# A gated linear attention and gMLP kernel on one core: constants made by separate operations, more engines per operation, a full-row bias matmul, and another order table

## The chip, the core and the metric

One Trainium2 chip, one of its cores. The core has five engines that run their own instruction queues in order and wait for one another by semaphores: TensorE (PE in the profile, its weight loads PEld), VectorE (DVE), ScalarE (ACT), GpSimd (POOL) and SyncE (SP), which here issues almost all DMA transfers. The metric is the device time of one execution in microseconds (us), as the median of several runs; lower is better.

## What is computed

Two stages follow each other. The first is a recurrence over time for 4 batches and 8 heads, 768 steps, head size 48; the second a gated MLP with a matmul along the sequence.

```python
# q, k, v, alpha: (4, 8, 768, 48)
for t in range(S):
    state = alpha[:, :, t, :, None] * state + np.einsum('bhd,bhe->bhde', k[:, :, t], v[:, :, t])
    y[:, :, t] = np.einsum('bhd,bhde->bhe', q[:, :, t], state)
x = y.transpose(0, 2, 1, 3).reshape(B, S, H * D)          # (4, 768, 384)
h = np.maximum(x @ w_in, 0.0)                             # w_in: (384, 1024)
u, v = h[..., :512], h[..., 512:]
v_n = (v - mean(v)) / np.sqrt(var(v) + 1e-06)             # over the last axis
v_s = np.einsum('ts,bsd->btd', w_spatial, v_n) + b_spatial[None, :, None]   # 768 x 768
out = (u * v_s) @ w_out                                   # w_out: (512, 384)
```

## The kernel before

**Chunks.** Each batch's 768 steps are cut into 6 chunks of 128, so there are 24 chunks, numbered 0 to 23 through all batches. Inside a chunk the recurrence is done as masked attention: logarithm of alpha (`ln`), cumulative sums by a matmul with a triangle of ones (`cum`), exponentials of both signs (`einv`, `eexp`), products with k (`kt`) and q (`qt`), transposes of both (`tr`, `trk`) and copies out of PSUM (`ev`, tile kqT), scores (`sc`), the causal mask (`m`, tile ptm), and the output `y`; across chunks a state is carried by `upd`, `z`, `S` and `sb` (tile sbd). The result is copied (`xs`), transposed (`xt`) and copied again (`xe`). Chunks 0 to 7 are taken in pairs, two steps to a partition (`pair`, lines 423 to 632: `lnp`, `cump`, `einvp`, `ktp`, `qtp`, `vbp`, `updq`, `ya`); the others one by one (`first`, from line 634).

**The MLP.** For every chunk `v` (three matmuls of 512 columns), statistics (`bn`), `rs` (two small activations) and `vn`; for each half batch (`th`) and quarter of the features (`ft`, `dsl`) `u` (three matmuls of 384 columns), `s` (six matmuls with the transposed spatial weights, in two parts of three), then an add of the bias on DVE and the gate `g`; for each of 6 row tiles `o` (four matmuls) and its store. The last `s` of all starts with a matmul that puts the bias row into PSUM, so that its gate reads PSUM directly. In two cases (`ACT_STATS`: batch 1 chunks 4 and 5, batch 2 chunks 2 and 3) the statistics are on ACT, by sums and squares. The weights are loaded as float32, cast by any engine (`cast`), the spatial ones transposed (`wt`) and copied out (`we`).

**The order is written out.** The program first lists operations without emitting them: each call of `op` appends one, with the engines that may run it and a price for each, the operations it depends on and a priority. `dma` appends two, the issue and the transfer. Then `replay` walks the string `PLAN`: a word such as `D56` emits operation number 56 of that list on DVE; letters are P, D, A, G (POOL), S (SP) and Q (the transfer, which emits nothing). Each engine's queue is therefore the order of its words. Numbers after colons on a P word are columns of matmuls on a constant tile `junk`, run on the operation's PSUM bank ahead of it; they compute nothing that is used. PSUM is handed out as a ring of 8 banks in the order of the P words. The prices, priorities and dependencies served whoever wrote the table; at run time only the order and the semaphores count, which the framework derives from the tiles that are read and written.

**Constants.** Four operations make them: `consts` (all of `constants`, on POOL by name, but with part of its instructions on DVE), `cz 0` and `cz 1` on DVE, `cz 2` on POOL. On POOL that gives le_pair, lt_pair (the triangles for pairs), ident, mask2 in that order, and later mask4 and ut_ones, which the single chunks use.

Of the kernel before, what the change touches and what calls it, by code (L numbers as in the profile page):

```python
# [36 lines left out]
class Slot:  # L37
# [5 lines left out]
    "kt": {"POOL": 0.9},  # L43
    "vb": {"POOL": 0.48, "ACT": 0.42},
# [6 lines left out]
    "o": {"ACT": 0.4},  # L51
# [6 lines left out]
S34 Q35 S36 Q37 G32 G0 Q33 S38 Q39 S94 Q95 S40 Q41 A42 P53:512:512:192 A54 D1 D2 D56 P43 S96 Q97 S98 Q99 S100 Q101  # L58
S163 Q164 S4 Q5 S165 Q166 S167 Q168 P59:464 G58 G48 A44 A45 A55 D46 D57 D47 P249:304 P49 P61 A50 P51 D52 D60 A62 A102
A250 P71:304 P74 P113 P103 D72 D73 D76 D75 P63 P77:172 D65 A114 D116 P119:148 A104 A64 A115 A105 A78 G66 G67 G106 D107  # L60
D117 D68 P79 P81 P111 P121 P247 P109 G3 G69 A108 A82 A80 D120 D122 D112 D110 P83 A84 A171 D248 S169 Q170 S9 Q10 S307
Q308 P131 P134 D133 D136 D132 D135 G70 G118 P172:228 P182 P123:240 A183 A8 A173 A124 P137 P138 A139 A174 G7 G6 D125
P85 G126 D128 D185 G127 G129 G175 P88 P142 P140 A86 A184 D176 D186 A143 A89 P188 P190 P180 P144 P178 A141 A191 A145
A181 P146 G11 G12 S309 Q310 S311 Q312 D130 D87 D179 D90 D189 P157 A187 A177 A158 A147 A13 P197 P200 P192 D199 D201
D198 D194 D202 P151:196 P155 A315 A193 A91 P326 P316 A327 P203 P153 P204 G195 G196 G329 A317 A328 A318 P149 A205 A154
D159 D156 D152 D330 G319 P208 P334 A209 P206 D320 P332 P324 P210 P322 D92 D335 D325 D333 D148 A207 P212 A211 A150 P347
P215 P221 A213 A160 A222 A216 S14 Q15 P223 P227 S18 Q19 D93 D323 D161 D348 D349 D214 G16 G17 A224 A228 P225 P229 A226
A21 P232 A234 D231 D230 D233 G20 P235:300 P238 S313 Q314 G331 G321 P344 P336 S367 Q368 S369 Q370 S22 Q23 S371 Q372
A237 A236 D217 D162 D346 A240 D338 A239 A218 D219 D220 A375 A337 P251 P263 P259 P376 A377 A378 G339 P264 D345 D341
D265 P260 D261 P255 P252 A380 A25 A24 D381 D253 P256 D257 G340 G342 G379 S409 Q410 S373 Q374 S446 Q447 S411 Q412 S413  # L70
Q414 S415 Q416 S26 Q27 S480 Q481 S448 Q449 S482 Q483 S450 Q451 S484 Q485 P383 A385 A417 S452 Q453 S577 Q578 S486 Q487
S581 Q582 S579 Q580 S583 Q584 P244 P241 P350 A246 D384 D245 D242 D243 P390 P354 P418 D392 D391 A351 A355 G262 G343
A420 A382 G254 G266 P279 P352 P271 P356 P393 P272 A353 A357 A419 G421 A422 A394 P280 P361 P386 P275 P395 A362 A424
A396 A31 D273 D423 D281 D387 P425 D397 D427 D426 D363 G282 G388 P276 P358 D277 P398 G258 G389 G278 G30 A399 A454 A359
A28 A488 P405 P432 P267 P455 P401 A402 A457 A456 D29 P291 P489 P268 A490 A459 D406 D433 D400 D434 D360 P283 P428 D269
D460 A492 D429 D493 G458 G491 P435 A284 A292 A436 G274 G461 G270 G430 G431 S648 Q649 S617 Q618 S650 Q651 S611 Q612
S652 Q653 S613 Q614 S690 Q691 S615 Q616 S694 Q695 S654 Q655 S692 Q693 P287 P462 P437 P495 P403 D463 D464 D497 D496
A288 A439 A438 P440 A585 A441 A364 D404 P469 P498 P295 P465 P586 P303 D471 D470 D466 D500 D499 A296 A587 A588 A590
A304 P299 G494 G467 G468 G589 G592 D591 D442 P472 A473 P501 P407 P474 A502 A300 P503 P593 P596 A443 A505 A408 D475
D476 P477 A478 D504 D366 D594 D595 D445 D444 D597 D365 P506 P600 P515 D601 D516 A507 A479 A508 D509 D602 A656 A510  # L80
A619 P517 P525 P513 P519 P529 P657 P533 P620 D511 D512 P526 P530 A514 A659 A658 A621 A661 A622 A698 A624 D518 D520
D527 D531 D662 P545 P534 P699 A701 A700 A703 D625 G598 G599 G660 G626 G623 G528 D535 P546 D547 P630 P627 P664 P537
P603 D631 D665 D704 G548 A629 A628 G632 G663 A604 P538 P634 P605 S728 Q729 S762 Q763 S696 Q697 S730 Q731 S732 Q733
S764 Q765 S766 Q767 D539 A607 A666 A606 D635 D636 P541 P667 P542 G702 G532 P706 P671 D668 D543 D673 D672 G669 G536
G670 G544 G633 P608 P637 P521 A707 A736 A708 A638 P737 P713 P639 P522 P549 D714 D715 D641 D523 A770 A609 A705 A738
A739 G740 A640 A741 D742 P771 P550 P642 A772 P709 P744 A774 A643 A746 D710 D551 D775 D745 D644 G524 S858 Q859 S734
Q735 S929 Q930 S860 Q861 G773 G711 G552 G712 G743 G540 P716 P674 A717 A675 P561 P718 P676 P777 P553 A562 A678 A677
D719 D779 D720 D610 P679 P751 A778 A554 A866 A680 A645 A681 P780 D752 P747 D748 D753 D781 D782 P682 P867 P721 P754
A868 A869 A871 A722 A755 S768 Q769 S862 Q863 A723 A776 D683 D872 P573 P688 P684 G749 G750 G870 P756 P874 D646 D757
D875 D685 D758 A689 A574 D724 A876 P686 P783 P569 P881 A784 P785 A570 A787 A687 A725 D882 D786 D883 P759 P557 A760  # L90
P788 P565 P796 P798 P800 S1042 Q1043 S971 Q972 S892 Q893 S864 Q865 S898 Q899 S896 Q897 A979 A558 A789 A566 A937 A900
S894 Q895 S935 Q936 G873 S975 Q976 S931 Q932 S933 Q934 S973 Q974 S977 Q978 S1008 Q1009 S567 Q568 S1046 Q1047 S559 Q560
S1012 Q1013 S1010 Q1011 S1044 Q1045 S1014 Q1015 D727 D647 D761 D726 P794 P806 D790 A791 D799 D797 D795 D792 D793 D801
P901 P980 P802 P938 P877 P807 A902 A903 A907 A905 A981 A939 A940 A982 A944 A984 P810 P803 A942 G904 D878 G941 G879
D808 D906 D804 G805 G880 G809 G983 D985 D943 P822 P884 P811 D812 A885 P823 P908 P886 P945 D824 P814 P911 P815 D912
D909 D816 G813 G817 G913 G825 A910 A887 A888 A947 A946 P889 A1016 A890 P952 P915 P987 D953 D916 D954 P830 P1017 P831
P818 A988 A1019 A1050 A1018 D917 P948 P819 P1051 D949 A1021 A986 A989 D1022 D832 G950 P834 A1052 G951 G1020 P990 P842
P918 A835 A1054 D820 D991 D1055 A843 A919 P838 P1024 P994 P920 D1025 D921 D995 D996 A839 A1023 G914 G833 G1053 G992
S1048 Q1049 S575 Q576 S836 Q837 S844 Q845 S293 Q294 S289 Q290 S571 Q572 S305 Q306 S301 Q302 S555 Q556 A922 A1026 S297
Q298 S285 Q286 S840 Q841 P826 P955 P827 D828 A956 P1057 P957 P1031 D958 P1027 D1028 D1033 D1032 P997 P923 A1058 A1059  # L100
A959 P969 P1060 A1056 A998 P999 D1062 D1001 D1061 D970 G821 G829 G993 G1029 A1000 A924 P960 P846 P1034 A961 A847 G1030
P1063 A1035 A1064 P1002 P963 P1036 P1065 D925 D891 A1003 D962 D1066 P850 P967 A1067 A1037 D1004 A926 D928 P1068 A964
A1038 P1039 D927 D968 A851 A1005 A1069 A1040 D1006 D1041 D1007 D1070 P965 P854 P1076 P1080 P1078 P1074 D966 A1079 A855
A1071 A1081 D1075 D1072 D1073 D1077 P1094 P1082 P1106 P1086 P1083 P1098 P1095 P1090 P1102 P1087 P1107 P1091 P1103
P1110 P1099 P1111 D1096 D1084 G1085 D1088 D1097 D1108 D1092 D1093 G1089 P1113 D1104 G1109 G1105 D1112 D1100 D1101
P1117 P1121 S852 Q853 S563 Q564 S856 Q857 S848 Q849 A1114 S1115 Q1116 A1118 P1133 S1119 Q1120 A1122 P1125 A1134 S1123
Q1124 P1129 S1135 Q1136 A1126 P1137 S1127 Q1128 A1130 A1138 S1131 Q1132 S1139 Q1140
# [16 lines left out]
def kernel(  # L124
# [113 lines left out]
    def constants(_):  # L238

        nc.vector.memset(junk, 0.5)  # L240
        nc.gpsimd.memset(le_pair, 0.0)
        nc.vector.memset(mask2[:, 0].bitcast(FP32), 0.0)
        zero_padding(lap_bufs[0])
        nc.vector.memset(ones_col, 1.0)
        nc.vector.memset(halves_of, 0.0)
        for ci in range(2):
            nc.vector.memset(halves_of[64 * ci:64 * ci + 64, ci:ci + 1], 1.0)
        nc.vector.memset(lt_pair.bitcast(FP32), 0.0)
        for t, base in ((le_pair, 0), (lt_pair, 1)):
            nc.gpsimd.affine_select(  # L250
                out=t, in_=t, compare_op=ALU.is_gt, fill=1.0, base=base, channel_multiplier=1,
                pattern=[[-1, 128]],
            )
            nc.gpsimd.memset(t[0:64, 64:128], 0.0)
        for t in (ktp_bufs[0], qtp_bufs[0]):
            zero_padding(t)
        make_identity(nc, ident)
        nc.vector.memset(mask2[:, 1].bitcast(FP32), 0.0)
        for par in range(2):
            for ci in range(2):  # L260
                rows = slice(64 * ci, 64 * ci + 64)
                nc.gpsimd.affine_select(
                    out=mask2[rows, par], in_=mask2[rows, par], compare_op=ALU.is_gt, fill=1.0,
                    base=par, channel_multiplier=2, pattern=[[0, 4], [-1, 2], [-2, 64]],
                )
# [891 lines left out]
```

## Time and profile before

| | us |
|---|---|
| median of 3 runs (143.01 to 143.22) | 143.06 |
| the profiled execution | 143.08 |
| its span in the profile | 141.3 |
| TensorE busy | 133.2 |
| DVE busy | 118.3 |
| ACT busy | 108.6 |
| POOL busy | 83.4 |

The span runs from the first to the last instruction; the rest of the execution's time lies around it. Busy is the time in which at least one instruction of that engine was running; TensorE's matmuls overlap, and their ends are modelled, so a busy TensorE need not be at its peak rate. A line such as "L828 PE MATMUL bank<-vn ... x192 | 36.8, 326" names the line of the program, engine, operation, what is written and read, the count, the busy time of all and the mean of one in ns; that mean is longer than the time from one start to the next where instructions overlap. L828 is the helper of all large matmuls, L197, L199, L203 and L205 those of copies and relu.

### The profile page before, as it was taken

Reading aid. Unit: us, or ns where it says so; the run is one execution under the profiler, and the core shown is the slowest. Engines: PE = TensorE matmul, PEld = TensorE weight load, DVE = VectorE, ACT = ScalarE, POOL = GpSimd, SP = SyncE. Lnnn points to the kernel's source line nnn. Section 1 sums busy time; section 2 is a strip of 40 time slices with the busy share of each in tenths; the row PEclk is TensorE's granted clock in tenths of the full one; section 3 lists DMA queues with packets and bytes.
Section 4 is the critical chain, followed back from the end, with each engine's and each line's share of the span. In section 5 each row is a group of like instructions: output and inputs, shape, how many; then the busy total and the mean of one; then the engine's idle time right before and its main releaser. Section 6 shows DMA issues by size and latency. Waiting matters only on the chain.

```text
span 141.3 us, 4968 instructions
## 1 busy us (share of the span) xinstructions
PE 133.2 (94%) x1912; PEld 84.2 (60%) x1923; DVE 118.3 (84%) x291; ACT 108.6 (77%) x282; POOL 83.4 (59%) x146
## 2 busy tenths in 40 slices
PE   7989798999999999999999999999999989999990
PEld 3457575575667656565675665656666656566560
DVE  7479878999989599999998898989979779894940
ACT  3677569988989969889887999997889969940061
POOL 6722986293449596982299899500799993000720
PEclk9999999999999999999999999999999999999999
DMA  4999999999898989989799999979978690112044
GB/s 102 323 323 332 331 272 311 225 320 238 241 232 156 283 161 208 205 161 212 154 205 179 193 217 177 222 143 195 250 151 203 225 375 24 70 56 102 0 164 170
DMA packets 89000, 28.64 MB, mean 203 GB/s; under 512 B 83728, under 2 KB 87440, under 8 KB 88976
## 3 DMA queue, kind: packets, MB, share of 16 engines
q1 hardware_dynamic: 88944, 28.32, 81.6%
q8 instruction: 15, 0.25, 0.7%
q14 instruction: 9, 0.07, 0.2%
q0 software_dynamic: 32, 0.00, 0.0%
HBM read 23.60 MB, written 4.72 MB: 200 GB/s over the span
## 4 chain that ended last, share of the span: by engine, by line
PE 71%; DVE 9%; POOL 7%; issue 5%; ACT 4%; ACTq 0%; POOLq 0%; DVEq 0%
PE bank L828 47%; PE bank L187 4%; DVE ptm L594 3%; PE bank L719 2%; PE bank L754 2%; POOL sbd L199 2%; POOL gT L989 2%; PE bank L511 2%; PE bank L782 2%; DVE ptm L765 2%; PE bank L740 1%; PE bank L583 1%; POOL kt L690 1%; PE bank L666 1%; DVE kqT L199 1%
## 5 line engine op out<-in xcount | busy, mean ns | idle before, releaser
L828 PE MATMUL bank<-w_spT,vn 128*128 128x384 bf16 x192 | 36.8, 326 | 0.0
L989 POOL TENSOR_TENSOR gT<-vsb,uT 128x384 bf16<-128x384 f32 x28 | 25.7, 923 | 14.9 <-DVE vsb L976 14.4
L690 POOL TENSOR_TENSOR kt<-kc,binv 128x384 bf16<-128x384 f32 x16 | 14.6, 914 | 13.4 <-ACT bc L685 8.6
L765 DVE TENSOR_TENSOR ptm<-bank,mask 128x512 bf16<-128x512 f32 x32 | 20.7, 682 | 1.9 <-PE bank L398 1.2
L828 PEld LDWEIGHTS <-vn 128*128 128x128 bf16 x192 | 16.6, 97 | 9.5 <-issue 0.2
L976 DVE TENSOR_TENSOR vsb<-bank,bsp_bc 128x384 f32<-128x384 f32 x31 | 16.5, 551 | 4.2 <-PE bank L828 2.5
L828 PE MATMUL bank<-xT,w_in 128*128 128x384 bf16 x96 | 18.7, 326 | 0.0
L828 PE MATMUL bank<-w_out_sb,gT 128*128 128x384 bf16 (+1 forms) x100 | 18.7, 319 | 0.0
L828 PE MATMUL bank<-w_in,xT 128*128 128x512 bf16 x61 | 17.2, 379 | 0.8 <-issue 0.2
L344 POOL TENSOR_TENSOR state<-state,bc 128x192 f32<-128x192 f32 x20 | 10.4, 520 | 11.4 <-DVE state L337 5.4
L197 ACT COPY kqT<-bank 128x512 bf16<-128x512 bf16 x21 | 12.1, 599 | 3.9 <-PE bank L719 1.1
L199 POOL CAST sbd<-state 64x192 bf16<-64x192 f32 x38 | 13.3, 350 | 2.0
L893 DVE BATCH_NORM_STATS2 stats<-v_sb 128x6 f32<-128x512 bf16 x20 | 13.7, 683 | 0.3 <-ACT v_sb L203 0.3
L203 ACT ACTIVATE v_sb<-bank 128x512 bf16<-128x512 f32 x20 | 11.8, 605 | 1.4 <-PE bank L828 1.3
L197 ACT CAST x_sb<-bank 128x384 bf16<-128x384 f32 x24 | 11.4, 490 | 1.5 <-PE bank L623 1.3
L828 PEld LDWEIGHTS <-w_in 128*128 128x128 bf16 x96 | 8.8, 97 | 5.9
L828 PEld LDWEIGHTS <-gT 128*128 128x128 bf16 x100 | 8.9, 97 | 5.6 <-DVE gT L989 0.4
L199 DVE COPY kqT<-bank 128x512 bf16<-128x512 bf16 x27 | 10.5, 416 | 1.9 <-PE bank L511 1.0
L187 PE MATMUL bank<-junk 128*128 128x512 f32 (+9 forms) x24 | 10.2, 529 | 1.1 <-DVE junk L240 1.1
L594 DVE TENSOR_TENSOR ptm<-bank,mask 128x512 bf16<-128x512 f32 x16 | 10.2, 683 | 0.5 <-PE bank L583 0.4
L197 ACT COPY xT<-bank 128x192 bf16<-128x192 bf16 (+1 forms) x26 | 9.4, 379 | 1.6 <-PE bank L398 1.1
L197 ACT COPY o_sb<-bank 128x384 f32<-128x384 f32 x9 | 4.4, 484 | 8.0 <-PE bank L828 8.0
(126 smaller groups left out, 284.0 us busy)
## 6 DMA issues: line engine op xcount, KB each, us to landing
ac<-in_alpha_dram SPq DMA_DIRECT2D x16, 192.0 KB, 4.1
kc<-in_k_dram SPq DMA_DIRECT2D x16, 192.0 KB, 4.8
qc<-in_q_dram SPq DMA_DIRECT2D x16, 192.0 KB, 4.1
vc<-in_v_dram SPq DMA_DIRECT2D x16, 192.0 KB, 3.8
raw_w<-in_moe_w_spatial_dram SPq DMA_DIRECT2D x3, 768.0 KB, 6.8
out_dram<-raw_w SPq DMA_DIRECT2D x11, 192.0 KB, 2.5
out_dram<-o_sb SPq DMA_DIRECT2D x9, 192.0 KB, 1.8
ac<-in_alpha_dram SPq DMA_DIRECT2D x4, 384.0 KB, 5.0
```

The costliest lines, as they stand in the source:

```text
L187: nc.tensor.matmul(out=flat[:, 0:cols].rearrange("p (a b) -> p a b", a=4), lhsT=junk, rhs=junk[:, None, 0:n].to_broadcast([128, 4, n]), st ...
L197: nc.scalar.copy(out=out, in_=in_)
L199: ENG[eng].tensor_copy(out=out, in_=in_)
L203: nc.scalar.activation(out=out, in_=in_, func=AF.Relu)
L344: ENG[eng].tensor_tensor(out=st["state"], in0=st["state"], in1=st["bc"][:, :, None].to_broadcast([128, HP, D]), op=ALU.mult)
L594: nc.vector.tensor_tensor(out=st[f"ptm{par}"][:, s], in0=st[f"pt{s}{par}"], in1=mask2[:, par], op=ALU.mult)
L690: ENG[eng].tensor_mul(out=k_blocks(kt3)[:, :, :, 0:D], in0=quad(st["kc"]), in1=st["binv"])
L765: nc.vector.tensor_tensor(out=st["ptm"][:, s], in0=st[f"pt{s}"], in1=mask4, op=ALU.mult)
L828: return lambda ps: nc.tensor.matmul(out=out(ps), lhsT=lhsT(), rhs=rhs(), start=start, stop=stop)
L893: nc.vector.bn_stats(out=stats, in_=d["v_sb"][:, tt, :])
L976: nc.vector.tensor_tensor(out=hold["vs"], in0=ps[:, 0:TH], in1=bsp_bc[:, th, :], op=ALU.add)
L989: ENG[eng].tensor_tensor(out=bt[b]["gT"][:, dsl, cols], in0=hold["vs"], in1=bt[b]["uT"][:, dsl, cols], op=ALU.mult)
```

## The change

Four things are edited, and the order table is replaced as a whole. The two lumps of constants become 20 operations of their own, each with the things that need it as its dependants (the diff shows a few of these dependencies). More engines may run `kt`, `vb`, `o`, `xs`, `g`. The last bias matmul multiplies the identity with the bias already spread over 128 rows (`bsp_bc`), and so waits for that copy. The numbers of operations move by up to 15, so that the two tables can't be compared word by word.

```diff
 ENGINES = {
-    "kt": {"POOL": 0.9},
-    "vb": {"POOL": 0.48, "ACT": 0.42},
+    "kt": {"POOL": 0.9, "DVE": 0.47},
+    "vb": {"POOL": 0.48, "ACT": 0.42, "DVE": 0.27},
...
-    "o": {"ACT": 0.4},
+    "o": {"ACT": 0.4, "DVE": 0.47},
 }
...
 PLAN = """
-S34 Q35 S36 Q37 G32 G0 Q33 S38 Q39 S94 Q95 S40 Q41 A42 P53:512:512:192 A54 D1 D2 D56 P43 S96 Q97 S98 Q99 S100 Q101
...
+D0 S49 Q50 D17 D13 S109 Q110 G47 Q48 D5 S53 Q54 G10 D7 S51 Q52 D2 D3 D11 G18 D15 D12 D1 S55 Q56 A57 G14 S111 Q112 G16
+P58:512:512:192 P264 A59 P68 A60 S113 Q114 G9 A69 D62 A70 D6 P66:512:232 S115 Q116 D71 P262 A67 D4 P74 A117 D61 S178
...
-    def constants(_):
-
-        nc.vector.memset(junk, 0.5)
...
+    def triangle(t, pattern, base=0, step=1):
+
+        nc.gpsimd.affine_select(
+            out=t, in_=t, compare_op=ALU.is_gt, fill=1.0, base=base, channel_multiplier=step, pattern=pattern)
...
+    def c_tri(_):
+        nc.gpsimd.memset(le_pair, 0.0)
+        for t, base in ((le_pair, 0), (lt_pair, 1)):
+            triangle(t, [[-1, 128]], base)
+            nc.gpsimd.memset(t[0:64, 64:128], 0.0)
+
+    def c_m2(par):
+
+        def emit(_):
+            for ci in range(2):
+                triangle(mask2[64 * ci:64 * ci + 64, par], [[0, 4], [-1, 2], [-2, 64]], par, 2)
+        return emit
...
-        op(("xs", i), "ACT", 0.38, xs, got(("y", i), ("xt", i - WK)), prio=P + 9, use=[st["sl_y"]])
+        op(("xs", i), {"ACT": 0.38, "DVE": 0.47}, None, xs, got(("y", i), ("xt", i - WK)), prio=P + 9, use=[st["sl_y"]])
...
-            op(("cump", j, par), "PE", 0.33 + 0.1, cum, got(("lnp", j)), prio=P + 2, take=sl_c[par], cols=768)
+            op(("cump", j, par), "PE", 0.33 + 0.1, cum, got(("lnp", j), ("c_tri",)), prio=P + 2, take=sl_c[par], cols=768)
...
-                lambda ps: ps[:, 0:TH], lambda: ones_row, lambda: b_sp_sb[:, th * TH:(th + 1) * TH], True, False))
+                lambda ps: ps[:, 0:TH], lambda: ident, lambda: bsp_bc[:, th, :], True, False))
...
-            op(("g", b, dsl, th), {"POOL": 0.9} if b < B - 1 else {"POOL": 0.9, "DVE": 0.69}, None, gm, got(("s", b, dsl, th)), prio=Q)
+            op(("g", b, dsl, th), {"POOL": 0.9, "DVE": 0.47}, None, gm, got(("s", b, dsl, th)), prio=Q)
...
-    op(("consts",), "POOL", 4.0, constants, prio=-10.0)
-    op(("cz", 0), "DVE", 1.7, zeros(0), prio=-5.0)
-    op(("cz", 1), "DVE", 0.7, zeros(1), prio=-4.0)
-    op(("cz", 2), "POOL", 1.2, zeros(2), [made[("consts",)]], prio=-3.0)
+    op(("c_junk",), "DVE", 0.17, lambda _: nc.vector.memset(junk, 0.5), prio=-20.0)
...
+    op(("c_m4",), "POOL", 0.95, c_m4, prio=-8.0 if PAIRS else -18.0)
+    op(("c_sbd",), "DVE", 0.62, c_sbd, prio=-9.5)
+    op(("c_row",), "DVE", 0.22, c_row, prio=-9.4)
...
+        op(("c_tri",), "POOL", 1.15, c_tri, got(("c_half",)), prio=-20.5)
```

Read back into operations (a pair or chunk behind the name, then the parity of the step; junk columns in brackets), the queues begin as follows. TensorE and POOL:

```
PE before:   cump 0.1 [512+512+192], cump 0.0, tr k 0.1 [464], bias 1 [304], tr k 0.0, tr q 0.1, tr q 0.0, sc 0.0 [304], sc 0.1,
             cump 1.1, cump 1.0, updq 0, ya 0 [172], tr k 1.1 [148], xt 0, y 1, tr q 1.0, tr q 1.1, bias 0, tr k 1.0, xt 1, sc 1.0
PE after:    cump 0.0 [512+512+192], bias 1, cump 0.1, tr q 0.0 [512+232], bias 0, tr k 0.1, cump 1.1 [492], cump 1.0, tr q 0.1,
             tr k 0.0, tr k 1.1 [512+108], sc 0.0, updq 0, tr q 1.0, tr k 1.0, sc 0.1, tr q 1.1, sc 1.1 [512+500], sc 1.0, ya 0
POOL before: b_sp issue, consts, vbp 0.1, vbp 0.0, S 0, sb 0, ktp 1.0, cz 2, S 1, sb 1, vbp 1.1, two casts of w_in
POOL after:  b_sp issue, c_m4, c_m2 1, c_tri, c_m2 0, c_id, ktp 1.1, vbp 0.0, ktp 1.0, S 0, vbp 1.0, sb 0, ktp 2.1, ktp 2.0,
             S 1, c_ut, sb 1, S 2, sb 2, vbp 2.0, S 3, sb 3, cast w_in, S 4, sb 4, cast w_in
```

DVE, ACT and the loads that SP issues:

```
DVE before:  cz 0, cz 1, ktp 0.1, ktp 0.0, qtp 0.1, qtp 0.0, ev q 0.0, ev k 0.1, four m of pair 0, z 0, ktp 1.1, qtp 1.0, ...
DVE after:   11 constants, qtp 0.0, c_qt, ktp 0.1, c_la, ktp 0.0, qtp 0.1, ev k 0.1, vbp 0.1, ev k 0.0, ev q 0.1, qtp 1.1,
             qtp 1.0, two m of pair 0, z 0, two m, z 1, two m of pair 1, two casts of w_in, two m, qtp 2.0, qtp 2.1, bn 0,
             z 2, ev q 2.1, ev q 2.0, z 3, bn 1, xs 2, xs 3, z 4, four m of pair 2, ...
ACT before:  lnp 0, einvp, einvp, eexpp, eexpp, ev k 0.0, ev q 0.1, lnp 1, bias copy 1, einvp 1.1, einvp 1.0, ebcp 0, ...
ACT after:   lnp 0, einvp, eexpp, einvp, eexpp, ev q 0.0, lnp 1, both bias copies, einvp 1.1, eexpp, einvp, eexpp, ev k 1.1,
             lnp 2, ebcp 0, ev q 1.0, ev q 1.1, ev k 1.0, vbp 1.1, cast w_in, xs 0, xs 1, einvp 2.1, ...
SP before:   ac0 kc0 qc0 ac2 vc0 kc2 qc2 vc2 ac4 w_in1 kc4 qc4 vc4 w_in0 ac6 kc6 qc6 w_sp0 w_sp1 vc6 ac8 kc8 w_sp2
SP after:    ac0 ac2 qc0 kc0 vc0 kc2 qc2 vc2 ac4 w_in1 kc4 qc4 vc4 ac6 w_in0 qc6 kc6 w_sp0 w_sp1 vc6 ac8 kc8 qc8 w_sp2
```

Over the whole kernel both tables have the same 24 `sc`, 64 parts of `s`, and so on; what differs is the engine of some 60 operations, the places, and the junk: 3572 columns before, 4312 after, the last of them ahead of the first `v` after the change.

## The prediction

> **What bounds the kernel now.** I read the page's busy shares first, then the table by stretches, then the timeline of the first 16 us, the chain of waits, and the answers for single tiles.
>
> ```profile
> span 141.3 us, 4968 instructions
> PE 133.2 (94%) x1912; PEld 84.2 (60%) x1923; DVE 118.3 (84%) x291; ACT 108.6 (77%) x282; POOL 83.4 (59%) x146
> ```
>
> The table by stretches:
>
> ```profile
> 10.00:15.00 5.00, 4.11 (x114) 3.28 (x105) 4.76 (x10) 3.45 (x10) 1.97 (x5) 1.00 1.13 332
> 15.00:20.00 5.00, 4.51 (x126) 3.40 (x123) 4.39 (x9) 3.44 (x8) 4.53 (x11) 1.00 1.05 297
> 40.00:60.00 20.00, 19.90 (x309) 12.55 (x309) 17.95 (x44) 16.91 (x44) 16.21 (x26) 1.00 0.97 204
> 120.00:138.00 18.00, 17.99 (x118) 10.23 (x109) 13.28 (x31) 7.45 (x22) 3.85 (x4) 1.00 0.22 81
> ```
>
> Columns after the stretch: length, then busy time of PE, PEld, DVE, ACT, POOL, granted clock, DMA share, GB/s. From 40 us on TensorE is covered all the time; before, it is DVE that is covered and TensorE has holes, some plugged with matmuls on `junk`. Busy time hides how far it is from full, so I lay TensorE's real work end to end. Prices are start-to-start times in its unbroken stretches:
>
> ```profile
> 69.99 1.97 PE bank L828 x12
> ...
> 120.12 17.56 PE bank L828 x105
> ```
>
> That is 0.164 us for a matmul of 384 columns (1.97/12); by other pieces of the same chain 0.22 for one of 512, 0.33 to 0.35 for a score operation, 0.23 for a transpose operation of k and q, 0.51 for `ya`, 0.78 for a full `updq`, 0.17 to 0.37 for `y`. All real operations together make 120.8 us. Taking an operation's start minus the work in front of it gives the time lost so far: 4.9 us at the first real matmul, 13.5 at 30 us, 15.0 at 44 us (`trk` of chunk 8), 16.9 at the last; then 3.6 us for the last copy, store and close. So the first 44 us lose 10.1 us after the start, and the 94 us behind them only 1.9. Only the head has much to give; the rest can lose more easily than win.
>
> ```profile
> 1.22 0.67 POOL L1101 DMA_DIRECT2D b_sp_sb<-in_moe_b_spatial_dram  x1 [0.78 <-POOLq L1141]
> ...
> 2.63 0.29 POOL L250 TENSOR_SCALAR_AFFINE_SELECT lt_pair<-lt_pair 128x128 bf16<-128x128 bf16 x1
> ...
> 3.58 2.82 POOL L262 TENSOR_SCALAR_AFFINE_SELECT mask<-mask 64x512 bf16<-64x512 bf16 x4
> ...
> 4.24 0.84 ACT L452 ACTIVATE la<-ac 128x768 bf16<-128x768 f32 x1 [2.22 <-DMA ac<-in_alpha_dram]
> ...
> 5.14 0.65 PE L461 MATMUL bank<-la,le_pair 128*128 128x384 bf16 x3
> ...
> 6.18 1.09 DVE L483 TENSOR_TENSOR kt<-kc,binvp 128x384 bf16<-128x384 f32 x2 [1.95 <-ACT binvp L469]
> ...
> 9.42 0.86 ACT L452 ACTIVATE la<-ac 128x768 bf16<-128x768 f32 x1
> ```
>
> The triangles are ready (3.1 us) long before the logarithm (5.1); the loads set the pace: landings by issue and time to landing are 4.2, 5.4, 6.6, 7.8, 9.1, 10.3, 11.5, 12.7, 14.1 us for the first nine, w_in's first half 17.2, its second 24.1.
>
> **Operations that change kind.** The constants are the same instructions regrouped. The last bias row is a matmul of 384 columns with 128 rows for one with 1 row: both take the columns' 0.164 us, and the rows of before are 0.331 (1 row) and 0.326 (128 rows) for one; zero. Counting the two tables: DVE gives up 7 copies of kqT (0.416), 9 relu (0.546), 2 kt (0.566), an sbd pair and a bias copy, -10.1 us, and takes 13 PSUM copies of o and x (0.548, the bsp_bc row), 4 more casts, 2 vb, a gate and small ones, +11.1. ACT +8.8 -9.5, POOL +3.5 -2.8. Totals hardly move (119, 108, 84 us), so the order decides. A weight cast on DVE is shown for 384 elements only (0.35); bounds for 512 are 0.35 and ACT's 0.61, for 768 0.35 and POOL's 0.83; I take 0.45 and 0.55, as 384 is faster there than on POOL (0.50). The five together: 1.75 to 3.7, taken 2.55.
>
> **The head, stepped through in the new order.** Each operation starts when its engine is free and its inputs are there, with the rows' start-to-start times (ACT 0.43 for 384, 0.49 for kqT; DVE 0.6 per mask, 0.54 kt, 0.48 qt, 0.36 kqT, 0.83 for statistics; POOL 0.91 kt, 0.5 state, 0.72 sbd) and about 0.1 between engines.
>
> 1. POOL runs b_sp's issue (to 1.9), mask4 (0.95), half of mask2 (1.41), and only then the triangles (1.25): 5.55. First real matmul 5.6 for 5.14, +0.5.
> 2. SP issues ac2 second and kc0 fourth: kc0 lands at 7.8 for 5.4. DVE's first kt starts at 7.85 for 6.18, +1.7, which swallows the 0.5. DVE's cover until then is the constants to 4.2 and one qt at 7.1.
> 3. On TensorE the transposes of kt of pair 1 stand ahead of the first scores. That kt is on POOL, behind ACT's two bias copies: 10.65 to 11.55. First scores 11.85 for 9.5, +2.3. Waiting behind: updq, both scores, so all masks of pair 0.
> 4. On ACT `lnp` of pair 2 stands ahead of pair 1's q copies and waits for ac4 (14.1): ACT idle 1.6 us. q copies end 15.95, scores of pair 1 start 16.05, masks of pair 1 end at 19.9 for 19.5. The 2.3 are nearly made up, since pair 1's k and q work was done beside pair 0's.
> 5. DVE then starts pair 2's qt at 20.3 for 21.3, a lead of 1.0; but five operations not there before (2 statistics early, 2 x copies, 1 z) stand ahead of pair 2's masks: end 28.1 for 28.4. `ya` of pair 2 starts near 28.2 with 14.63 of work done: lost 13.6, as before.
> 6. w_in's second half goes one place later (25.3 for 24.1); one of its casts is on POOL behind two sbd pairs: done 28.0 for 27.0. Behind it SP holds w_sp's second third (28.1 for 27.1, landing 35.0 for 33.9) and vc6, ac8, kc8. The third transpose of w_sp waits for that and a cast on DVE: 35.75, lost 15.1; before 14.8 at the same operation.
> 7. DVE has three w_sp casts, two statistics and three transposed-weight copies ahead of the last masks and the first qt of chunk 8: 43.0 for 42.9, where TensorE, with less work by then, waits 0.55; the scores of chunk 8 start near 44.5, lost 16.1 for 15.05. Sum of the head: **+1.0 us**; bounds -0.8 and +2.2 from the DVE casts at either end and 0.1 either way on some ten hand-overs.
>
> **Behind the head.** In batch 1 ACT does the statistics of chunks 4 and 5. After the last v matmul of chunk 5 its queue holds v (0.5), two squares (0.75 each), three u (0.4), two logarithms (0.43), the rstd pair (0.52): 4.6 us, then two vn (0.7). TensorE has 5.1 us of work until it needs them, so 0.3 is missing, 0.4 with a hand-over; before it had 4.2 us for 3.0 plus 0.7. **+0.4**, bounds 0 and +1. At the end the last gate is on POOL (0.92) after a 0.55 add, with 1.97 us of output matmuls ahead of its user; it fits if DVE's gate before it isn't held up:
>
> ```profile
> L989 POOL TENSOR_TENSOR gT<-vsb,uT x28: 908/914/1157, 43.2 to 134.4; 128x384 bf16<-128x384 f32 x28
> L989 DVE TENSOR_TENSOR gT<-vsb,uT x3: 549/559/1093, 131.2 to 135.2; 128x384 bf16<-128x384 f32 x3
> ```
>
> The same gate took 0.55 and 1.09 on DVE and up to 1.16 on POOL. Held up once, the end slips 0.2; I take 0. The Trainium skill, "SBUF — State Buffer", section "Who interferes with whom", says that a DVE instruction with two SBUF inputs and a POOL instruction reading SBUF block each other; the spread in these rows agrees; by that rule the slip would be certain, 0.2 more.
>
> Junk after the first real matmul is 3096 columns for 2356, some 1.0 us more at 0.73 per 304 and 0.94 per 464; it lies in waits of steps 2 to 4 (TensorE stands there 5 us), worth up to 1.0 if those vanish.
>
> **Sum.** Profiled execution 143.08 us (span 141.3 and 1.8 around it; the median of the runs is 143.06): +1.0 +0.4 = 144.5, rounded down to **144.4** for lead I may have missed.
>
> **Rivals.** (a) *The lead is kept.* In step 5 DVE is 1.0 us ahead; if pair 2's masks end by 27.1, TensorE keeps it, and with step 6 no later than before and w_sp's rows not held by the buffer, as the third transpose is before (it stood 1.0 us), the head comes out at -1.5: 141.6. For: the constants are thinner, DVE casts w_in. Against: w_in's second half lands later. It decides at the masks of pair 2. (b) *Nothing to see:* gain and loss meet, 143.1. (c) *The tight order tears behind the head.* In the new table's stretches of 6 us of TensorE work, by the rows' prices, ACT is handed 6.9 and 8.1 us in two running, DVE 7.8 in another; before the worst are 6.7 and 6.8. 15.0 in 12 us is 3.0 too many; if two thirds show, 144.4 + 2 = 146.4. Against: ACT's neighbours hold 3.9 and 4.0. (d) That the constants, once on DVE in small pieces, hold up ACT's first logarithm: the last of them ends at 3.9 to 4.2 and ac at 4.2, so it costs 0 to 0.1; inside the forecast.
>
> **Chances.** Forecast (143.5 to 145.3) 0.43, (c) 0.17, (a) 0.29, (b) 0.11. The range 141.5 to 146.6 leaves out some 0.2, half at each end; the likeliest case alone 143.5 to 145.3. A measurement of this kernel tells about 0.2% (0.3 us) from no change: faster 0.29, same 0.11, slower 0.60.
>
> **What would show it.** Right: first real matmul near 5.6 and first scores near 11.9; ACT waiting for DMA ac near 14; TensorE waiting on w_row or its cast near 35; span near 142.6. Wrong: masks of pair 2 done before 27.2, or the u matmuls of batch 0 before 28; then (a) holds. A span over 144 with the waits between 60 and 80 us is (c).

## The result and the profile after

| | before | after |
|---|---|---|
| median, us | 143.05 (20 runs) | 142.63 (20 runs) |
| lowest, us | 143.00 | 142.12 |
| the profiled execution, us | 143.08 | 142.43 |
| its span, us | 141.3 | 140.6 |
| time lost at the first real matmul (start less work in front) | 4.9 | 5.2 |
| at 30 us | 13.5 | 13.9 |
| at `trk` of chunk 8 (starts at 43.3 in front, at 42.3 behind the change) | 15.0 | 15.0 |
| with 95 us of work done (111.5 us in both) | 16.4 | 16.4 |
| at the last matmul | 16.9 | 16.2 |

The ratio is 0.9953 (95% interval 0.9936 to 0.997): faster by 0.47%, where slower by 0.9% was forecast. A second timing of the changed kernel, beside other runs, gave 0.9924 (0.9898 to 0.995). Executions of one kernel spread upwards from their lowest time, here by 1.1 us before the change and by 2.0 behind it; the last section shows one source, and for small differences the lowest times stand beside the medians.

The page after, busy shares; then the table by stretches (length, busy PE, PEld, DVE, ACT, POOL, granted clock, DMA share, GB/s):

```profile
span 140.6 us, 4974 instructions
PE 135.3 (96%) x1921; PEld 84.1 (60%) x1921; DVE 118.5 (84%) x292; ACT 108.1 (77%) x279; POOL 83.9 (60%) x148
```

```profile
10.00:15.00 5.00, 5.00 (x106) 3.81 (x105) 3.65 (x9) 3.94 (x10) 2.23 (x3) 1.00 1.11 327
15.00:20.00 5.00, 5.00 (x87) 2.66 (x86) 4.19 (x9) 4.60 (x11) 2.42 (x5) 1.00 1.07 296
40.00:60.00 20.00, 19.96 (x311) 12.78 (x310) 17.83 (x44) 15.41 (x37) 17.60 (x30) 1.00 0.97 204
120.00:138.00 18.00, 17.35 (x109) 10.33 (x107) 13.46 (x30) 6.40 (x18) 3.89 (x4) 1.00 0.35 130
```

TensorE looks fuller from 10 to 20 us (5.00 and 5.00 for 4.11 and 4.51) and has gained nothing there: junk fills the holes. In the last row it is busy for 17.35 us, since the end has come nearer. The timeline of the head:

```profile
4.28 0.84 ACT L443 ACTIVATE la<-ac 128x768 bf16<-128x768 f32 x1 [2.26 <-DMA ac<-in_alpha_dram]
...
5.06 0.29 POOL L241 TENSOR_SCALAR_AFFINE_SELECT lt_pair<-lt_pair 128x128 bf16<-128x128 bf16 x1
...
5.60 0.11 PEld L452 LDWEIGHTS <-lt_pair 128*128 128x128 bf16 x1 [0.34 <-POOL lt_pair L273]
...
8.01 0.56 DVE L474 TENSOR_TENSOR kt<-kc,binvp 128x384 bf16<-128x384 f32 x1
```

The triangles are late and TensorE waits for them, and the first `kt` starts at 8.01 for 6.18: the steps forecast for this part are there. So in these two executions the head was slower up to 12 us of work (time lost some 13 for 12.3) and level at `trk` of chunk 8, and the gain of the profiled pair is all behind 111 us.

One execution of each kernel is a narrow base for the head, since the start differs from run to run (last section). Over the five traces with the changed order up to there (after, E2, E7, E13, E15) some 14.6 to 15.2 us are lost at `trk` 8, over the seven with before's order (before, E1, E3, E5, E6, E11, E12) 15.0 to 16.0. The new head is not slower there, and may be a little faster.

The part of the trace of before that the gain comes from: its chain of waits (start, length, what), a few lines above the one quoted in the prediction, the matmul that this chain releases, and the last 6 us:

```profile
109.93 0.92 POOL kt L690
111.72 0.92 POOL gT L989
112.64 0.88 POOL kt L690
```

```profile
113.57 0.29 PE L719 MATMUL bank<-ident,kt 64*128 64x64 bf16 x8 [0.34 <-POOL kt L690]
```

```profile
130.39 3.00 POOL L989 TENSOR_TENSOR gT<-vsb,uT 128x384 bf16<-128x384 f32 x3 [12.51 <-DVE vsb L976]
...
132.01 0.09 PEld L828 LDWEIGHTS <-ones_row 1*128 1x128 bf16 x1 [0.32 <-issue]
132.01 0.33 PE L828 MATMUL bank<-b_sp_sb,ones_row 1*128 1x384 bf16 x1
132.27 1.25 PEld L828 LDWEIGHTS <-vn 128*128 128x128 bf16 x9 [0.17 <-issue]
132.28 1.64 PE L828 MATMUL bank<-w_spT,vn 128*128 128x384 bf16 x9
...
132.72 1.09 DVE L989 TENSOR_TENSOR gT<-vsb,uT 128x384 bf16<-128x384 f32 x1
...
135.85 1.91 PEld L828 LDWEIGHTS <-gT 128*128 128x128 bf16 x16 [0.38 <-DVE gT L989]
```

Three losses. `kt` of chunk 23 stands on POOL behind a gate of batch 2, and TensorE waits for it from 113.2 to 113.57. Around the 1-row bias matmul the weight loads stand for 0.32 and 0.17 us. Three gates start late on POOL, beside them a gate on DVE takes 1.09 instead of 0.55, and TensorE waits 0.38 for the last gate. The last batch after the change:

```profile
130.21 0.91 POOL L980 TENSOR_TENSOR gT<-vsb,uT 128x384 bf16<-128x384 f32 x1 [1.55 <-DVE vsb L967]
...
130.51 0.10 PEld L819 LDWEIGHTS <-ident 128*128 128x128 bf16 x1
...
130.68 2.37 PEld L819 LDWEIGHTS <-vn 128*128 128x128 bf16 x15
...
133.11 4.01 PEld L819 LDWEIGHTS <-gT 128*128 128x128 bf16 x28
```

No weight load here waits for anything. The chain of waits names the first of the three losses, by POOL; the other two have no row in it.

### The profile page after: what moved, and what is told of

It reads as the page before. It is cut to its first block, busy times and chain, and to the rows that moved or that the text cites. A ratio compares the mean times of both kernels' runs of the same rounds, so it can differ in the third digit from the quotient of the medians.

```text
span 140.6 us, 4974 instructions
## 1 busy us (share of the span) xinstructions
PE 135.3 (96%) x1921; PEld 84.1 (60%) x1921; DVE 118.5 (84%) x292; ACT 108.1 (77%) x279; POOL 83.9 (60%) x148
## 4 chain that ended last, share of the span: by engine, by line
PE 59%; ACT 9%; DMA 9%; SPq 7%; POOL 5%; DVE 5%; issue 4%; ACTq 0%; POOLq 0%
PE bank L819 42%; SPq L432 7%; DMA raw_w<-in_moe_w_in_dram 5%; DMA ac<-in_alpha_dram 3%; PE bank L710 3%; PE bank L745 2%; PE bank L773 2%; PE bank L731 2%; PE bank L657 2%; PE bank L767 1%; POOL kt L681 1%; DMA out_dram<-raw_w 1%; PE bank L389 1%; POOL kt L474 1%; ACT vn L880 1%
## 5 line engine op out<-in xcount | busy, mean ns | idle before, releaser
L819 PE MATMUL bank<-w_spT,vn 128*128 128x384 bf16 x192 | 35.9, 326 | 0.0
L980 POOL TENSOR_TENSOR gT<-vsb,uT 128x384 bf16<-128x384 f32 x27 | 25.0, 939 | 12.5 <-DVE vsb L967 12.1
L819 PEld LDWEIGHTS <-vn 128*128 128x128 bf16 x192 | 17.3, 97 | 10.2
L681 POOL TENSOR_TENSOR kt<-kc,binv 128x384 bf16<-128x384 f32 x16 | 14.6, 917 | 11.9 <-ACT bc L676 7.3
L819 PE MATMUL bank<-xT,w_in 128*128 128x384 bf16 x96 | 19.9, 326 | 0.0
L819 PE MATMUL bank<-w_in,xT 128*128 128x512 bf16 x72 | 18.8, 379 | 0.3 <-ACT xT L198 0.2
L198 ACT COPY kqT<-bank 128x512 bf16<-128x512 bf16 x28 | 15.9, 598 | 2.2 <-PE bank L710 1.5
L884 DVE BATCH_NORM_STATS2 stats<-v_sb 128x6 f32<-128x512 bf16 x20 | 13.6, 682 | 0.0
L204 ACT ACTIVATE uT<-bank 128x384 bf16<-128x384 f32 x23 | 10.9, 492 | 2.2 <-PE bank L819 2.0
L188 PE MATMUL bank<-junk 128*128 128x512 f32 (+6 forms) x22 | 10.7, 613 | 1.1 <-DVE junk L1050 1.1
L585 DVE TENSOR_TENSOR ptm<-bank,mask 128x512 bf16<-128x512 f32 x16 | 10.3, 682 | 1.0 <-PE bank L574 1.0
L198 ACT CAST x_sb<-bank 128x384 bf16<-128x384 f32 x19 | 9.0, 494 | 2.3 <-PE bank L773 2.3
L916 DVE TENSOR_SCALAR vn<-v_sb,mvs,rstd 128x512 bf16<-128x512 bf16 x24 | 8.9, 404 | 1.5 <-ACT rstd L909 1.5
```

The lines of the kernel that those rows point to most:

```text
L188: nc.tensor.matmul(out=flat[:, 0:cols].rearrange("p (a b) -> p a b", a=4), lhsT=junk, rhs=junk[:, None, 0:n].to_broadcast([128, 4, n]), st ...
L198: nc.scalar.copy(out=out, in_=in_)
L204: nc.scalar.activation(out=out, in_=in_, func=AF.Relu)
L585: nc.vector.tensor_tensor(out=st[f"ptm{par}"][:, s], in0=st[f"pt{s}{par}"], in1=mask2[:, par], op=ALU.mult)
L681: ENG[eng].tensor_mul(out=k_blocks(kt3)[:, :, :, 0:D], in0=quad(st["kc"]), in1=st["binv"])
L819: return lambda ps: nc.tensor.matmul(out=out(ps), lhsT=lhsT(), rhs=rhs(), start=start, stop=stop)
```

## The experiments

Orders are shown as the parts of an engine's queue that change; `g`, `s` and `o` carry the batch, then the quarter of the features and the half batch (`g`, `s`) or the row tile (`o`). "End loss" is the time lost between the second part of `s` 2.3.1 (it starts at 106.6 us in both kernels; the recorded expectations call it `s` 1.2.3.1) and the last matmul of all, by the prediction's prices, from one trace each. By it before has +0.42 and after -0.24. The sign comes from prices a little too high; differences count, to some 0.1, and to 0.15 where the operations just ahead of the cut differ.

**E1, the last batch's order alone, in before.**

```diff
-POOL: g 3.0.0, g 3.1.0, g 3.2.1, g 3.1.1     DVE: g 3.3.0, g 3.2.0, g 3.3.1, g 3.0.1
+POOL: g 3.2.0, g 3.0.0, g 3.3.0, g 3.1.1     DVE: g 3.1.0, g 3.0.1, g 3.3.1, g 3.2.1, and three copies of o
```

> The kernel before, with the s, g, o, output-store and last-bias operations of batch 3 alone put in the order and on the engines of the changed kernel. Theory T (the gain is in the last batch: its gates start earlier on POOL and none of DVE's is held up; before loses 0.65 us between 95 us of TensorE work and the last matmul, after loses none): 142.5 to 142.6 us for 143.05, the DVE gates all near 0.55 us and TensorE's lost time at the last matmul 16.3 for 16.9. Rival H (the gain comes from the head or from the whole table): 143.05, lost time still 16.9. Half of it (0.25 to 0.35) would say that the rest of before's tail loss sits at trk 23 near 113.5 us, which this edit doesn't touch.

143.16 median, 142.91 lowest for 143.01 (ratio 0.9998, 0.998 to 1.0016). DVE's gates are all 0.55, the wait for the last gate is gone, and yet only some 0.1 is won; end loss +0.31. Theory T falls as it was put.

**E2, the reverse, in after** (`s` and `o` go with the gates, as in E1).

```diff
-POOL: g 3.2.0, g 3.0.0, g 3.3.0, g 3.1.1     DVE: g 3.1.0, g 3.0.1, g 3.3.1, g 3.2.1, and three copies of o
+POOL: g 3.0.0, g 3.1.0, g 3.2.1, g 3.1.1     DVE: g 3.3.0, g 3.2.0, g 3.3.1, g 3.0.1
```

> The changed kernel, with the same operations of batch 3 put back in the order and on the engines of the kernel before; all else as changed. Theory T: 143.0 to 143.2 us, as slow as before, with one DVE gate near 1.1 us and waits of PE for gates in the last 12 us. Rival H: 142.6, as the changed kernel.

142.91 median, 142.53 lowest (0.9979, 0.9954 to 1.0003): 0.3 to 0.4 over the changed kernel, end loss +0.14. The same order is worth 0.3 to 0.4 here and 0.1 in before, so something else of the change goes with it.

**E3, all code edits, the order of before.**

```diff
-consts, cz 0, cz 1, cz 2
+the constants as separate operations (19; the section on the change says 20), in the same order and on the same engines
-last bias matmul: ones_row (1 row) x b_sp_sb
+last bias matmul: ident (128 rows) x bsp_bc
```

> All edits of the code (constants as separate operations, engines on offer, full-row bias matmul) with the order and engines of before; only the last bias matmul differs in what it reads. Theory T: 143.05 us (142.9 to 143.2), since the table alone moves the time. Rival E (the edits themselves pay, by the thinner constants or the 128-row bias matmul): 142.6 to 142.8. If the full-row matmul waits for its bias copy: 143.2 or more.

143.15 median, 143.01 lowest (1.0002, 0.998 to 1.0023). But its trace differs at the end; the weight loads, the bias matmul and the next, and the gates:

```profile
132.17 0.10 PEld L819 LDWEIGHTS <-ident 128*128 128x128 bf16 x1
132.34 0.33 PE L819 MATMUL bank<-bsp_bc,ident 128*128 128x384 bf16 x1
...
132.50 1.63 PE L819 MATMUL bank<-w_spT,vn 128*128 128x384 bf16 x9
...
133.13 1.09 DVE L980 TENSOR_TENSOR gT<-vsb,uT 128x384 bf16<-128x384 f32 x1
...
136.26 0.77 PEld L819 LDWEIGHTS <-gT 128*128 128x128 bf16 x8 [0.57 <-DVE gT L980]
```

The stop at the 1-row weights (0.32) is gone, and the wait for DVE's last gate has grown from 0.38 to 0.57: DVE's chain, not TensorE's, sets the end in this order, so an earlier TensorE only waits longer. What the full-row matmul saves is hidden behind the order of the gates.

**E5, one word: `kt` of chunk 23 ahead of a gate, in before.**

```diff
-POOL: kt 22, sb 19, g 2.3.1, kt 23, S 21
+POOL: kt 22, sb 19, kt 23, g 2.3.1, S 21
```

> The kernel before with one word moved: on POOL, kt of chunk 23 stands ahead of the gate of batch 2 (features 3, half 1) that stood in front of it. Theory S (two separate losses near the end, one of 0.35 us at trk 23, one of 0.1 to 0.4 in the last batch): the wait of PE for POOL kt (0.34 at 113.6 us) goes, and undisturbed runs take 142.7 us for 143.02. Rival W (the whole order between chunks 19 and 23 is needed; a shorter wait at one transposition comes back at the next): 143.0.

142.82 median, 142.80 lowest, seven of twelve runs within 0.02 of that, for 143.04 to 143.07 (0.9981, 0.9959 to 1.0004). That is 0.24 by the lowest times, of the 0.34 that the profile gives the wait. End loss +0.18.

**E6 and E7, the tables spliced at 106.6 us:** E6 has before's order up to there and the changed one behind it, E7 the reverse; both with the changed code.

> The code of the changed kernel, with before's order up to the last matmul of s.1.2.3.1 (106.6 us in both traces, with 16.45 and 16.47 us lost) and the changed order from there. Theory S: all of the gain lies behind the cut: undisturbed runs 142.3 to 142.45, median 142.5, lost time at the last matmul 16.2 less what the start of the run loses differently. Rival H (the changed order gains in the head where TensorE is warm early, which the one profiled execution hides): 142.6 to 142.8.

> The reverse: the changed order up to the same matmul, before's order from there. Theory S: undisturbed runs 142.8 to 143.0, that is 0.65 over the changed kernel's 142.12 to 142.4, median near 143.2; waits of PE for POOL kt near 113 us and for gates in the last 12 us, as before. Rival H: 142.3 to 142.5.

E6: 142.59 median, 142.24 lowest (0.994, 0.9914 to 0.9965), end loss -0.39; by the medians the whole gain is there with the old head; by the lowest times 0.1 to 0.2 is left for the new one (142.12 and 142.03 in the changed kernel's two timings). E7: 143.41 and 143.27 (1.0004, 0.9984 to 1.0024): slower than the changed kernel by 0.8, not told from before by the medians and 0.23 above it by the lowest. Its end loss is +0.99, half of it at the first operations behind the splice: an order that fits one front does not fit another.

**E11, E1 and E5 together; E12, E11 with the 128-row bias matmul; E13, after with the 1-row one.**

```diff
 E13, in the changed code:
-lambda ps: ps[:, 0:TH], lambda: ident, lambda: bsp_bc[:, th, :], True, False))
+lambda ps: ps[:, 0:TH], lambda: ones_row, lambda: b_sp_sb[:, th * TH:(th + 1) * TH], True, False))
```

> The kernel before with the edits of e1 (s, g, o of batch 3 as after the change) and e5 (kt of chunk 23 ahead of a gate) together. If the two losses add up: 0.11 + 0.25 = 0.36, lowest 142.66 to 142.70. If each hides a part of the other, as e2 suggests (the last batch's order was worth 0.41 there for 0.11 in e1): lowest 142.25 to 142.4, median 142.6, as e6.

> The kernel of e11 (before, with the last batch's s, g, o as after the change and kt of chunk 23 ahead of a gate) with the code edits of the change, so that the last bias matmul has 128 rows. Theory R (the 1-row matmul itself costs: in the trace of before its weight load stands 0.32 us with nothing to wait for and the next one 0.17, where the 128-row one of the changed kernel takes its turn in 0.17; the start of the s group behind it comes 0.25 us later): 142.66 - 0.25 = 142.41 lowest, median 142.55. Rival O (order alone): as e11, lowest 142.66, median 142.82. What then is missing to e6's 142.24 (0.17) would lie at y 23 to v 3.3 near 119 us, where e11's trace has 0.17 more than e6's.

> The changed kernel with its last bias matmul put back to one row (ones times the bias row); order and all else as changed. Theory R: 0.25 us more, as no gate waits behind it in this order: lowest 142.37, median 142.9, a gap of 0.3 us at the weight load of the 1-row matmul. Rival O: as the changed kernel, 142.12 and 142.63.

E11: 142.82 median, 142.66 lowest (0.9973, 0.995 to 0.9995): the two add up, 0.33 by the lowest times and 0.35 by the end loss (+0.07). E12: 142.73 and 142.53 (0.9958, 0.9932 to 0.9984): 0.13 more by the lowest, 0.21 by the end loss (-0.14 for +0.07), under the 0.25 expected. E13: 142.51 and 142.24 (0.994, 0.9911 to 0.9969), beside the changed kernel's 142.35 and 142.03 on the same chip: 0.2, and its trace has the stop back, at the weight loads of the last `s`:

```profile
130.45 0.09 PEld L819 LDWEIGHTS <-ones_row 1*128 1x128 bf16 x1 [0.32 <-issue]
...
130.71 2.23 PEld L819 LDWEIGHTS <-vn 128*128 128x128 bf16 x15 [0.17 <-issue]
```

So the end's 0.81 (from +0.42 to E6's -0.39) is 0.24 for `kt` 23, 0.11 for the gates' order, 0.21 for the full-row bias matmul once that order is there, and 0.25 that E12 doesn't have; of that its trace shows 0.18 between `y` 23 and `v` 3.3, where TensorE waits for the copies of the transposed result, and 0.10 between two `v`. That last quarter is read from traces, not tried by itself.

**E4, E8, E9, E10, E14: can the head's waits be taken away?** All have the changed code and the changed order behind the head.

```diff
 E4: -POOL: c_m4, c_m2 1, c_tri, c_m2 0, c_id, ktp 1.1   +POOL: c_tri, c_id, c_m2 0, c_m2 1, ktp 1.1, ..., c_m4 beside c_ut
     -SP: ac0 ac2 qc0 kc0   +SP: ac0 kc0 qc0 ac2
     -PE: tr k 1.1 [512+108], sc 0.0, ..., sc 1.1 [512+500]   +PE: sc 0.0, tr k 1.1 [512+108], ..., sc 1.1 [228]
     -ACT: lnp 2, ebcp 0, ev q 1.0, ev q 1.1, ev k 1.0   +ACT: ebcp 0, ev q 1.0, ev q 1.1, lnp 2, ev k 1.0
     -DVE: c_half, c_kt 1, c_col, ..., c_mz 0   +DVE: c_kt 1, c_half, c_mz 0, c_col, ...
 E8: as E4, but POOL c_tri, c_id, c_m2 1, c_m2 0, c_m4, ktp 1.1; c_mz 0 in its old place; no junk on tr k 1.1; lnp 2 behind ev k 1.0
 E9: E8, w_in0 behind qc6 and kc6      E10: after, w_sp0 ahead of qc6 and kc6      E14: E8, w_sp0 ahead of qc6 and kc6
```

> The changed kernel with the four waits of its head taken away by order: the triangles first on POOL, key chunk 0 loaded second, pair 1's q copies ahead of pair 2's logarithm on ACT, the first scores ahead of the transposes of pair 1's k, and 784 junk columns fewer. First real matmul 5.1 for 5.6, first scores near 10 for 12.5. Theory M (the mark at 44 us, the transposes of chunk 8, is set by the weights' landings and DVE's queue, so that time won before it is lost again there): 142.6 us, lost time at trk 8 15.0 as now, more waits of PE for w_row between 33 and 36 us. Rival C (a lead in the head is carried to the end): 141.6 to 142.0, lost time at trk 8 14.0 to 14.4.

E4: 144.23 median (1.0074, 1.004 to 1.0108), 1.6 us slower than after. The edit had faults of its own: mask4 stands late on POOL ahead of sbd 1, pair 1's k copy behind the logarithm, 620 junk columns behind the first scores. By 28 us it has lost 2.1 us more than the changed kernel, and 2.1 are still missing at the last matmul: here lateness in the head is carried whole.

> The changed kernel with the waits of its head taken away anew, without the three faults of the first try: POOL makes the triangles first and mask4 last before its idle time; k and q of chunk 0 are loaded second and third; pair 2's logarithm stands behind all three copies of pair 1; the first scores stand ahead of the transposes of pair 1's k, with no junk between; 1404 junk columns fewer. First scores 11.7 for 12.5, scores 1.0 at 15.9 for 17.0. Theory C (a lead in the head is carried, as the lateness of e1 and e3 was carried whole): lost time at trk 8 14.3 for 15.0, undisturbed runs 141.6, median 142.0. Theory M (the weights' landings set the mark at 44 us): trk 8 15.0, time as the changed kernel, with TensorE waiting at the transposes of w_sp near 34 us.

> The kernel of e8 with the load of w_in's second half put behind those of q and k of chunk 6. In the traces of e4 and e8 TensorE stands 0.65 and 1.04 us between the same two instructions (its 705th and 706th) with nothing to wait for, 1.5 us after a 16 KB block of queue 8 (instructions) that was read at 24.8 and 23.5 us; in the trace of the changed kernel that block is read at 20.8. Theory I (the block of TensorE's instructions queues behind the data loads, which e8 issues up to 2.4 us earlier): with a shallower queue the block is read by 22 us, the stall at the 705th instruction goes, lost time at trk 8 is 14.5 to 14.9, and the runs are less spread: lowest 141.8 to 142.1, median 142.3. Rival P (the lead of the head itself makes TensorE run into the block whatever the loads do): stall and times as e8, median 143.0.

> The changed kernel with one load moved the other way: the first third of w_sp (768 KB) ahead of q and k of chunk 6, so that some 2.4 us more of data stand in front of the same block of instructions. Theory I: the block is read at 22.5 to 24.5 us, TensorE stalls at its 705th instruction by 0 to 1.0 us, median 142.9 to 143.4 with a wide spread. Rival P: no stall there; 142.6, unless q or k of chunk 6 come late, which would show as DVE or POOL waiting for DMA qc or kc near 28 us.

> The head of e8 with the load order of e10 (the first third of w_sp ahead of q and k of chunk 6). Theory J, new: TensorE's block of instructions waits behind loads of q and k in small packets, not behind bytes: over ten traces it is read at 20.8 to 21.5 us where q and k of chunk 6 are issued after about 20.0 us, and at 22.1 to 24.8 where they are issued before. Then here the block is read near 21, nothing stalls at the 705th instruction, and e8's lead (0.84 us over the changed kernel at 6 to 8 us of work) reaches trk 8: lost time 14.0 to 14.3, lowest 141.5 to 141.8, median 141.9. Rival N: the stall stays or another takes its place (w_in or w_sp late): 142.3 to 143.0, trk 8 at 14.6 or more.

E8, E9 and E14 do lead: their time lost at 6 us of work is 10.8, 10.3 and 10.2 for the changed kernel's 11.6 (11.3 in its second trace). At `trk` 8 they are behind it, 15.5, 15.8 and 16.1 for 15.0 (14.9); medians 143.04 (0.997, 0.9943 to 0.9998), 143.45 (1.0005, 0.9979 to 1.0031) and 143.06 (0.9973, 0.9945 to 1.0001). Each loses its lead at another transfer. The waits of the three (engine, line, what for: us in all, times, longest), E8 from 24 to 26.5 us, E9 and E14 from 26 to 33:

```profile
PEld L365 <- issue: 1.0, 1, 1.0
```

```profile
POOL w_in L200 <- DMA raw_w<-in_moe_w_in_dram: 2.2, 1, 2.2
...
PEld L819 <- POOL w_in L200: 1.6, 1, 1.6
```

```profile
DVE qt L481 <- DMA qc<-in_q_dram: 1.6, 1, 1.6
...
PE bank L819 <- DVE qt L481: 1.2, 1, 1.2
```

In E8 it is TensorE's own instructions (last section), in E9 the second half of w_in, in E14 q of chunk 6. E9's expectation held for the stall (the block of instructions was read at 22.1, nothing stood there) and failed for the time. E10's failed: 142.30 median, 142.04 lowest (0.9932, 0.9906 to 0.9957), no stall, block read at 21.3; more bytes queued in front did not make it late. Theory J, put up for E14, fell too: q of chunk 6 was issued at 19.8 there and the block read at 22.5, with no stall. In the five traces with the changed kernel's own loads (after, E2, E7, E13, E15) the block is read at 20.8 to 22.8, so one trace of each order can't tell what sets its time; that stays open. In the changed kernel the DMA share is 1.11 and 1.07 from 10 to 20 us: a lead in computation arrives at data that isn't there yet. That the transfers as a whole are the limit is what the three agree on, not a thing tried by itself.

**E15, the changed kernel again.**

> The changed kernel once more, on the same chip as e12 to e14, so that their times stand beside it. 142.63 median, 142.12 lowest, as in its first timing; if the chip moves it by more than 0.15, e10's gain over it (0.33 by the medians) is not told from that.

142.35 median, 142.03 lowest. The medians moved by 0.28 between two timings, so E10 (142.30, 142.04) is the same as the changed kernel, and no version here beats it.

## Why the prediction was wrong

**The step that failed** is the end: "I take 0" for the tail behind the head, and the reading that only the head has much to give. The end gives 0.65 us in the profiled executions, a third of the 1.9 that the prediction itself counted behind 44 us and never placed; the head, priced at +1.0, and batch 1's statistics, at +0.4, gave nothing. I read the last line of the chain (105 matmuls in 17.56) as the unbroken stretch to take prices from, and did not ask which operations inside the last 30 us started late. `kt` of chunk 23 stood further up in that chain, and TensorE's wait for it, 0.34, in the timeline; the two tables show that a gate was moved from in front of it. The chip gives 0.24 (E5).

**The full-row bias matmul**, priced at zero, is worth 0.2 where the gates don't hide it (E12, E13). The prediction compared busy lengths, 0.331 and 0.326; the price is in the time from one start to the next. The 1-row matmul starts 0.26 us after the matmul in front of it, and the next starts 0.27 behind it (132.01 to 132.28); with 128 rows both steps are 0.16 (132.34 to 132.50 in E3). That is 0.1 on the way to one row and 0.1 on the way back. It is not a matter of the one row alone: in the trace of before, behind 45 us, 331 matmuls of 384 columns between two of 128 rows take 0.162 to the next start, and the 14 whose next has 64 or 48 rows take 0.258. The Trainium skill, "TensorEngine Tiling (Array Packing)", section "Key Properties", says that a change of tiling mode drains TensorE. The traces agree with a price for changing the rows; that it is a drain no trace here shows.

**The gates.** The prediction had the 1.09 row and the rule for it (the Trainium skill, "SBUF — State Buffer", section "Who interferes with whom") in hand. It used them to ask whether the changed kernel could be held up, and not what they cost the kernel before. The changed order gives 0.11 by itself (E1) and the 128-row matmul alone 0.0 (E3); together they give 0.32 (end loss -0.14 in E12 for +0.18 in E5). The slip of 0.2 that the rule made certain did not show: in the changed kernel all gates on DVE take 0.55 to 0.56, and no weight load waits for one; the gates on POOL take up to 1.32.

**The head**, forecast at +1.0, measured 0.0 in the profiled executions. Steps 1 to 5 came within 0.7 us, most within 0.3: the first real matmul at 5.3 (5.6 forecast), the first `kt` at 8.01 (7.85), first scores 12.5 (11.85), the logarithm of pair 2 at 14.08 (14.1), masks of pair 1 done at 20.3 (19.9) and of pair 2 at 28.2 (28.1), 13.8 lost at `ya` of pair 2 (13.6). Steps 6 and 7 were mis-sized: the transpose that waits for w_sp's second third came at 35.1 (35.75 forecast), 14.5 lost for 15.1, and the first qt of chunk 8 at 41.6 (43.0), so that the scores of chunk 8 started at 43.5 (44.5) and had lost 15.1 for 16.1. The forecast gave that third 6.9 us to land; it landed in 4.3, the quickest of the three (median 5.5).

**Batch 1's statistics**, forecast at +0.4, did not show as a wait: between 64 and 80 us no matmul of either trace waits for `vn` or for the statistics. The changed kernel does lose 0.2 to 0.6 more there, between 58 and 63 us of work, at transposes and scores of chunks 13 to 15 that wait for POOL's `kt` and ACT's copy, and is level again at 70 us of work (16.20 in both).

**Two sums of the prediction are off**, without weight in the forecast. The 740 more junk columns are 1.5 to 1.8 us by the rows it names (0.94 for 464, 0.73 for 304), not 1.0. Rival (a), 141.6, leaves out the +0.4 of the statistics.

**The rivals.** (a), faster because the head's lead is kept, has the right sign and mostly the wrong mechanism: in the profiled pair there is no lead at 44 us, and E6 has the gain without the new head. (c), the tight order tearing between 60 and 80 us, did not show. The chance of 0.29 for faster lay wholly on (a); a rival that asks what the change repairs at the end was missing.

## What to carry to other kernels

Place every microsecond that the kernel before loses, stage by stage to its last store, before pricing a change: what a change repairs is in the old trace, not in the diff. When two engines take turns in setting the end, an edit on one of them can show nothing alone (E3: 0.0) and its full worth beside the other (E12: 0.2), so an edit that "does nothing" is tried again beside the others. A change of the number of rows between matmuls has a price of its own; look at the time from start to start, not at the busy lengths. A lead gained under a DMA share near 1.1 was lost at the next transfer that was late; moving one transfer only passed the wait to another.

## What the runs showed of the hardware

**TensorE starts at half pace, and how long is up to the run.** The first matmuls of 384 columns, before and E1 (start, length, matmul, count):

```profile
5.14 0.65 PE L461 MATMUL bank<-la,le_pair 128*128 128x384 bf16 x3
5.62 0.33 PE L461 MATMUL bank<-la,lt_pair 128*128 128x384 bf16 x1
```

```profile
5.27 1.17 PE L461 MATMUL bank<-la,le_pair 128*128 128x384 bf16 x3
6.23 0.53 PE L461 MATMUL bank<-la,lt_pair 128*128 128x384 bf16 x1
```

They follow each other after 0.16 us in the one and 0.32 in the other, with the same program up to there and a mean granted clock of 1.00 in both executions. The full pace began between 4.4 us (E15) and some 7 (E1, E11) in the traces. E1 had lost 0.6 more than before by then and 0.6 more at the last matmul (17.4 for 16.9, with E1's own gain of 0.1 in it). So the start is one source of the spread of the runs, and a lowest time tells more here than one trace. The Trainium skill, "TensorE: Matmul & The Clock Gate", section "Part 1: The HAM clock gate (the "warmup" mystery)", states half rate at first, a free-running window and a start that varies by run. The traces agree with the half rate and the variation; the window itself no trace here shows.

**Changing the rows of a matmul costs TensorE 0.1 us.** With 384 columns the time to the next start is 0.162 us when the next matmul has 128 rows too and 0.258 when it has 64, 48 or 1 (before, behind 45 us; 0.162 and 0.259 in the changed kernel); with 512 columns it is 0.216 and 0.312. Some 60 such changes, to fewer rows or back, lie behind 15 us in either kernel, between the transposes and scores of the chunks and the MLP's matmuls. By these figures that is some 6 us in all, an estimate; the prediction's work and time lost hold it without showing it by itself. No run here puts the chunks' matmuls together to save it.

**TensorE can wait for its own instructions.** In E4 and E8 it stands 0.65 and 1.04 us between its 705th and 706th instruction, in the middle of one operation and waiting for nothing the profile shows. Queue 8 brings fifteen blocks of 16 KB over the same DMA engines as the loads; the second was read from 24.8 and 23.5 us on in those two (0.9 us long) and from 19.4 to 22.8 on in the fifteen other traces, and the stall ended 1.5 and 1.4 us after the read's end. The Trainium skill, "Runtime: NRT & Kernel Launch", section "Instruction fetch mechanics", has blocks of 256 instructions fetched ahead, the cost mostly hidden; in these two traces, under a DMA share of 1.04 to 1.18 from 22 to 26 us, it wasn't.
